# A bigger ring of exp buffers and a moved fold chunk in a kernel of attention and a spectral filter

## The chip, the cores and the metric

One core of a Trainium2 chip runs the whole program. The metric is the device time of one execution in microseconds (us). The time before is the median of three runs, 407.62 us (407.6 to 410.17). The five engines (TensorE or PE, VectorE or DVE, ScalarE or ACT, GpSimd or POOL, SyncE or SP) run side by side, each in its own order of instructions; the order is written out when the program is built, and semaphores keep the engines in step.

## The reference

Two independent halves, written side by side into one output of 2048 x 896:

```python
# A: x [1, 2048, 448], 16 heads of 28
qkv = (x @ wqkv) split into q, k, v and heads
p = softmax(q @ k^T * 28 ** -0.5)          # 16 heads x 2048 x 2048
a = (p @ v, heads side by side) @ wo
# B: x [1, 2048, 448], w_r and w_i [2048, 225]
X = rfft2(x in float32) * (w_r + 1j * w_i)
b = irfft2(X, s=(2048, 448)) as bfloat16
out = concatenate([a, b], axis=-1)
```

## The kernel before, in words

**Attention.** The 16 heads stand in four groups g of four, the 2048 queries in four chunks n of 512. A *block* is a group with a query chunk (16 blocks); a block has 16 key chunks of 128, and a key chunk four heads. A *unit* is one head's 128 keys x 512 queries of scores: 1024 units. One unit is one matmul of `fill` (L1101) into one of the eight PSUM banks. Most units are exponentiated on ScalarE (`fill_act`, L1135), one, two or three adjacent banks by one instruction, into `ET`, a ring of `ESL` = 16 buffers; `e_alloc` (L987) gives out adjacent buffers, and four matmuls (`emit_pv`, L1237) that add one key chunk of all four heads to the block's accumulator free them. For some key chunks (`KDS`) VectorE may do the exp instead: it turns scores into an integer that, read as bfloat16, is nearly the exp (L1145, tile `T`), and makes three shifted copies of four such units at once (L1158, tile `TC`); TensorE then runs four PV passes for them in place of one. Such a set of four units is called a quad here. A job that runs on TensorE in several steps is finished before a PV step may follow.

**Ahead of it**, x is transposed on TensorE against an identity table (`cid`) into `xAT`, and q, k and V of each group are projected (`proj_qk`, `proj_v`); VectorE empties them into `qT`, `kT` and `Vaug`. The start (`head`, L1371 on) does that for the first 512 rows after a few warm-up matmuls (`warm`, L1368). The denominators travel through DRAM on SP's queue (`spread`, L1270): out, back transposed, reciprocal on VectorE, out, broadcast into `rzb` by four DMAs; GpSimd then multiplies (L1286) into `onrm`.

**The spectral half** folds x by its symmetries on GpSimd (`fold_chunk`, four chunks, `fold_edge`; all by the helper `tt`, L607), multiplies by tables `FR` along the rows (`s_job`) and `T1` along the columns (`x_job`), multiplies by the weights on GpSimd (`zmul_`), goes back along the rows (`i_job`, `combine`) and by table `T2` along the columns (`y_job`). The 16 output tiles of this half (`y_job`) and the 16 of attention (`o_job`, with `Wo`) are emptied by `store` (L1341) and sent out by SP or ACT.

**The order** is made by a planner at build time, which keeps a clock for each engine and costs for each operation. ScalarE's next fill goes first, then PV steps, then jobs by due time; `FILLER` and `FORCE` put idle matmuls (L969) where TensorE would rest. Work for VectorE and GpSimd is deferred with a due time (`defer`, `flush`). `rules` (L913) draws some limits (how far VectorE may be behind, `dve`; how far ahead of ScalarE to fill, `lead`) by the seeds in `PLAN`, one for each 32 units. `HPACE` paces the loads of B's x by units done. GpSimd's operations and VectorE's `TC` copies pass one token (`port=True`): each waits by a semaphore for the last of the other engine's.

Of the kernel before, what the change touches and what calls it, by code (L numbers as in the profile page):

```python
# [23 lines left out]
class Prog:  # L24

    def __init__(self, nc, sems):
# [97 lines left out]
    def dma(self, eng, fn, sem, reads=(), writes=(), kb=128, issue=0.6, past=()):  # L124
# [193 lines left out]
def build_kernel(nc, A_x, A_wqkv, A_wo, B_x, B_w_r, B_w_i, out):  # L318
    WARM = 9
# [22 lines left out]
    with ctx:  # L342
        sem_names = ["pe", "act", "dve", "pool"]
        sem_names += ["d_x%d" % i for i in range(4)] + ["d_w", "d_wq", "d_w2", "d_wv", "d_wo", "d_c", "d_t", "d_xe"]
        sem_names += ["d_n%d" % i for i in range(7)] + ["d_i"] + ["d_xr%d" % i for i in range(4)] + ["d_wr%d" % i for i in range(2)]
# [1369 lines left out]
```

## Time and profile before

| | |
|---|---|
| median of three runs | 407.62 us |
| the profiled execution | 408.68 us, of which 406.9 us span from first to last instruction |
| PE busy | 392.0 us (96%) |
| DVE busy | 323.0 us (79%) |
| ACT busy | 385.8 us (95%), of it 379.7 us exp |
| POOL busy | 168.0 us (41%) |
| granted TensorE clock | 0.999 of full speed |
| DMA | 18.09 MB, mean 44 GB/s |

Busy is the time in which an engine has an instruction running; an instruction that overlaps the next is longer than the distance between their starts. PE's time holds the idle matmuls of L969. ACT starts its exp at 9.36 us and the rest of its time, up to 395.5 us, is nearly all exp; behind it comes the end of the last block and the last output tiles.

### The profile page before, as it was taken

Reading aid. Unit: us, or ns where it says so; the run is one execution under the profiler, and the core shown is the slowest. Engines: PE = TensorE matmul, PEld = TensorE weight load, DVE = VectorE, ACT = ScalarE, POOL = GpSimd, SP = SyncE. Lnnn points to the kernel's source line nnn. Section 1 sums busy time; section 2 is a strip of 40 time slices with the busy share of each in tenths; the row PEclk is TensorE's granted clock in tenths of the full one; section 3 lists DMA queues with packets and bytes.
Section 4 is the critical chain, followed back from the end, with each engine's and each line's share of the span. In section 5 each row is a group of like instructions: output and inputs, shape, how many; then the busy total and the mean of one; then the engine's idle time right before and its main releaser. Section 6 shows DMA issues by size and latency. Waiting matters only on the chain.

```text
span 406.9 us, 15403 instructions
## 1 busy us (share of the span) xinstructions
PE 392.0 (96%) x6693; PEld 141.4 (35%) x6693; DVE 323.0 (79%) x593; ACT 385.8 (95%) x374; POOL 168.0 (41%) x154
## 2 busy tenths in 40 slices
PE   8899999989999999999999999999999999999997
PEld 4434333333322333342424433433222224323333
DVE  2477878776899889887886788788998888979744
ACT  3899999999999999999999999999999997999992
POOL 5266674756501012465557455745225350410010
PEclk9999999999999999999999999999999999999999
DMA  8613410010000004100001400000000010021033
GB/s 243 193 55 119 143 57 6 21 37 3 17 4 15 2 15 108 48 2 4 16 3 39 130 15 3 4 17 2 15 2 16 2 17 3 27 71 47 25 104 129
DMA packets 20813, 18.09 MB, mean 44 GB/s; under 512 B 9419, under 2 KB 19593, under 8 KB 20361
## 3 DMA queue, kind: packets, MB, share of 16 engines
q1 hardware_dynamic: 18104, 13.91, 11.7%
q0 software_dynamic: 320, 1.84, 1.5%
q10 hardware_dynamic: 2320, 1.35, 1.1%
q8 instruction: 53, 0.87, 0.9%
q14 instruction: 16, 0.12, 0.1%
HBM read 13.30 MB, written 3.79 MB: 42 GB/s over the span
## 4 chain that ended last, share of the span: by engine, by line
PE 48%; ACT 42%; issue 5%; DMA 2%; DVE 2%; POOL 0%; SPq 0%; ACTq 0%; DVEq 0%; POOLq 0%
ACT ET L1135 42%; PE PS L1101 14%; PE PS L458 13%; PE PS L1237 12%; PE PS L498 5%; PE PS L969 2%; DMA R1b<-in_B_w_i_dram 1%; DMA cid<-cst_id 1%; PE PS L476 1%; PE PS L1394 0%; POOL ptmp L607 0%; PE PS L1379 0%; DVE qT L509 0%; DVE wst L1349 0%; DVE TC L1158 0%
## 5 line engine op out<-in xcount | busy, mean ns | idle before, releaser
L1135 ACT ACTIVATE ET<-PS 128x1024 bf16<-128x1024 f32 (+2 forms) x364 | 379.7, 1220 | 7.1 <-PE PS L1101 5.2
L1145 DVE TENSOR_SCALAR T<-PS 128x512 int16<-128x512 f32 x196 | 132.5, 686 | 29.3 <-PE PS L1101 27.9
L1101 PE MATMUL PS<-qT,kT 28*128 28x512 bf16 x1024 | 141.1, 384 | 5.8 <-ACT ET L1135 2.5
L1158 DVE TENSOR_SCALAR TC<-T 128x2048 int16<-128x2048 int16 x147 | 94.0, 686 | 8.7 <-POOL ptmp L607 3.6
L1101 PEld LDWEIGHTS PS<-qT,kT 28*128 28x128 bf16 x1024 | 35.2, 90 | 127.8 <-ACT ET L1135 93.3
L1237 PE MATMUL PS<-ET,Vaug 128*32 128x512 bf16 x828 | 77.0, 384 | 1.6 <-ACT ET L1135 0.8
L1286 POOL TENSOR_TENSOR onrm<-oaug,rzb 128x512 bf16<-128x512 bf16 x15 | 17.4, 1157 | 86.6 <-DVE TC L1158 39.0
L1237 PE MATMUL PS<-TC,Vs 128*32 128x512 bf16 x588 | 51.5, 384 | 0.3 <-DVE TC L1158 0.2
L458 PE MATMUL PS<-T,R 112*32 112x225 bf16 (+5 forms) x776 | 38.8, 294 | 0.6 <-DVE qT L509 0.5
L498 PE MATMUL PS<-xAT,wst 112*28 112x512 bf16 x480 | 36.9, 382 | 0.4 <-ACT ET L1135 0.4
L607 POOL TENSOR_TENSOR R<-R1b 113x512 bf16<-113x512 f32 (+1 forms) x16 | 19.9, 1280 | 32.1 <-DVE R1b L775 32.1
L607 POOL TENSOR_TENSOR ptmp<-R1a,R1b 128x450 f32<-128x450 bf16 x24 | 23.0, 972 | 23.2 <-DVE TC L1158 13.9
L1237 PEld LDWEIGHTS PS<-ET,Vaug 128*32 128x32 bf16 x828 | 20.1, 94 | 31.5 <-issue 17.2
L1349 DVE CAST wst<-PS 128x448 bf16<-128x448 f32 x26 | 16.0, 620 | 11.8 <-PE PS L458 11.2
L458 PEld LDWEIGHTS PS<-T,R 112*32 112x32 bf16 (+3 forms) x776 | 17.2, 96 | 15.8 <-issue 9.7
L607 POOL TENSOR_TENSOR ptmp<-ptmp 128x450 f32<-128x450 f32 x16 | 18.1, 1144 | 9.7 <-DVE Vs L529 4.9
L607 POOL TENSOR_TENSOR R1a<-ptmp 128x450 bf16<-128x450 f32 x16 | 15.6, 980 | 14.8 <-DVE TC L1158 8.9
L458 PE MATMUL PS<-FR,R1b 128*32 128x512 bf16 (+3 forms) x256 | 21.3, 384 | 0.2 <-issue 0.2
L969 PE MATMUL PS<-cid 128*32 128x256 bf16 x436 | 20.9, 274 | 0.6 <-ACT ET L1135 0.2
L607 POOL TENSOR_TENSOR R1b<-onrm 128x896 bf16<-128x896 f32 x8 | 16.7, 2097 | 10.5 <-DVE TC L1158 6.7
L607 POOL TENSOR_TENSOR ptmp<-R1a 128x448 f32<-128x448 bf16 (+1 forms) x16 | 16.1, 1030 | 11.1 <-DVE Vs L529 5.8
L607 POOL TENSOR_TENSOR onrm<-ptmp 128x896 f32<-128x896 f32 x8 | 17.1, 2148 | 8.3 <-DVE TC L1158 4.6
(81 smaller groups left out, 321.2 us busy)
## 6 DMA issues: line engine op xcount, KB each, us to landing
FR<-cst_tab SPq DMA_DIRECT2D x3, 1024.0 KB, 4.9
out_dram<-wst SPq DMA_DIRECT2D x26, 112.0 KB, 1.7
rzb<-scr SPq DMA_DIRECT2D x60, 32.0 KB, 1.8
R<-in_A_x_dram SPq DMA_DIRECT2D x3, 448.0 KB, 4.5
R1a<-in_B_x_dram SPq DMA_DIRECT2D x2, 448.0 KB, 3.6
out_dram<-wst ACTq DMA_DIRECT2D x6, 112.0 KB, 2.1
wst<-in_A_wqkv_dram SPq DMA_DIRECT2D x2, 294.0 KB
R<-in_A_x_dram ACTq DMA_DIRECT2D x1, 448.0 KB, 5.1
```

What stands on the lines that cost most here:

```text
L458: ins = e.matmul(out[c:c1], lhsT[:, c:c1], rhs, start=start, stop=stop, tile_position=(0, c))
L476: f = lambda e, cc=cc, i=i, dlo=dlo: e.transpose(M.bitcast(BF16)[0:112, 512 * cc + 128 * i:512 * cc + 128 * i + 128], xa[:, n, i, dlo:dlo ...
L498: ins = e.matmul(M[32 * j:32 * j + DH], wst[0:112, c, off + DH * j:off + DH * j + DH], xAT[0:112, c, 512 * n:512 * (n + 1)], start=c == 0, ...
L607: P.defer(eng, lambda e: e.tensor_tensor(out, a, b, op), reads=reads, writes=writes, busy=c, allow=allow, port=True, after=after)
L969: ins = e.matmul(PS[32 * c:32 * c + 32, 512 * b + h:512 * b + h + 256], cid[:, 32 * c:32 * c + 32] if bks else zt[:, :], cid[:, 0:256], st ...
L1101: ins = e.matmul(bank(bk), kT[32 * j:32 * j + DH, g % 2, 128 * kc:128 * (kc + 1)], qT[32 * j:32 * j + DH, b % QSL, :], start=True, stop=Tr ...
L1135: P.op("act", lambda e: e.activation(dst, src, ACT.Exp, scale=ESC), reads=[("B", i) for i in o], writes=[("E", p + k) for k in range(n)], ...
L1145: P.defer("dve", lambda e, bk=bk, slot=slot: e.tensor_scalar(T0[:, slot, :], bank(bk), BIAS, 0.0, ALU.add, ALU.max), reads=[("B", bk)], wr ...
L1158: P.defer("dve", lambda e, c=c, m=m, s0=s0: e.tensor_scalar(TC[:, c - 1, 4 * m:4 * m + 4, :], T0[:, s0:s0 + 4, :], SHF * c, None, ALU.add) ...
L1237: ins = e.matmul(bank(bk)[32 * j:32 * j + 32, :], lh, rhs, start=first, stop=last, tile_position=(0, 32 * j))
L1286: P.defer("pool", lambda e: e.tensor_tensor(onrm[:, g, cs], oaug[:, i, :], rzb[:, :], ALU.mult), reads=[ko] + [("rzb", j) for j in range(4 ...
L1349: evac(lambda e: e.tensor_copy(astg[:, slot, :], M[:, 0:448]), mk, w, 448, 1.5, after=lambda: out_dma(row, slot))
```

## The change

1. The ring `ESL` has 24 buffers in place of 16.
2. The tables `T2` and `Wo` no longer have tiles of their own: they lie in `xAT`, and are loaded by `last_loads` when the last projection has been emptied. `rzb` is gone: the reciprocals are broadcast into `onrm`, where GpSimd multiplies them in place.
3. Of the four fold chunks one (`FOLDV`) is done by VectorE, in scratch tiles that lie in `FR`; the tables for `FR` are loaded when that chunk is done. VectorE's fold operations don't pass the token.
4. A's x is loaded with four consecutive rows in a partition (3584 B in a run) in place of one (896 B); output rows follow that order. The identity table is loaded first on ACT's queue in place of second on SP's. Warm-up: 8 matmuls in place of 9, on a broadcast column of `zt`.
5. A q or k tile that is among the next that the exp needs (`wanted`) is due for emptying at once (-3.0 in place of 1.0).
6. The planner: landing times are kept by semaphore; `dve` may be drawn from 1.0 to 4.0 in place of 2.0 to 3.0; up to two VectorE units in a fill (`ndf`) in place of one (`NDF`); new seeds; B's x is asked for at units 2 and 5 in place of 3 and 13.

```diff
-ESL = 16
+ESL = 24
...
+FOLDV = (3,)
+FALLOW = {"dve": 12.0, "pool": 12.0}
...
-HPACE = ((3, "x", 0), (5, "w", 1), (5, "x", 1), (5, "w", 0))
+HPACE = ((2, "x", 0), (3, "x", 1), (5, "w", 1), (5, "w", 0))
...
-    WARM = 9
+    WARM = 8
...
-        wo = sb("wo", [128, NG, 448])
...
-        T2 = sb("T2", [128, 2, 2, D])
...
-        rzb = sb("rzb", [128, 512])
...
+        T2 = xflat[:, 0:1792].rearrange("p (v b k) -> p v b k", v=2, b=2)
+        wo = xflat[:, 1792:3584].rearrange("p (g k) -> p g k", g=NG)
...
-            P.dma(q, lambda e, n=n: e.dma_start(xa[:, n], A_x[0][512 * n:512 * n + 512, :].rearrange("(c p) d -> p c d", p=128)),
+            P.dma(q, lambda e, n=n: e.dma_start(xa[:, n], A_x[0][512 * n:512 * n + 512, :].rearrange("(p c) d -> p c d", p=128)),
                   "d_x%d" % n, writes=[("xa", n)], kb=448)
         load_x(0)
-        P.dma("sp", lambda e: e.dma_start(cid[:, :], cst_h.ap()[:, :]), "d_c", writes=["cid"], kb=32)
+        P.dma("act", lambda e: e.dma_start(cid[:, :], cst_h.ap()[:, :]), "d_c", writes=["cid"], kb=32)
...
-                evac(fn, mk, [key] + ([("k", 0, "h")] if key == ("k", 0, 0) and g else []), 512, 1.0, after=lambda: done.add(nmk))
+                def after():
+                    done.add(nmk)
+                    last_loads()
+                evac(fn, mk, [key] + ([("k", 0, "h")] if key == ("k", 0, 0) and g else []), 512, -3.0 if nmk in wanted() else 1.0, after=after)
...
+        def last_loads():
+
+            if st.get("last") or any((k, NG - 1, n) not in done for k in "qkV" for n in range(4)):
+                return
+            st["last"] = True
+            xk = [k for n in range(4) for k in xkeys(n)]
+
+            def load_o():
                 for j in range(4):
                     P.dma("sp", lambda e, j=j: e.dma_start(wo[32 * j:32 * j + DH, :, :], A_wo.rearrange("(g j d) n -> j d g n", g=NG, j=4)[j]),
-                          "d_wo", reads=["wo"], past=rd, writes=[("wo", j)], kb=98)
+                          "d_wo%d" % j, reads=["wo"], writes=[("wo", j)], kb=98)
+            P.dma("sp", lambda e: e.dma_start(T2, t2_h.ap()[:, :].rearrange("p (v b k) -> p v b k", v=2, b=2)), "d_t", writes=["T2"] + xk, kb=448)
+            P.defer("pool", lambda e: e.memset(wo, 0.0), writes=["wo"] + xk, busy=1.6, allow=6.0, port=True, after=load_o)
...
-            P.defer(eng, lambda e: e.tensor_tensor(out, a, b, op), reads=reads, writes=writes, busy=c, allow=allow, port=True, after=after)
+            P.defer(eng, lambda e: e.tensor_tensor(out, a, b, op), reads=reads, writes=writes, busy=c, allow=allow, port=eng == "pool", after=after)
...
+        def folded():
+
+            st["folded"] = st.get("folded", 0) + 1
+            if st["folded"] == 2 * len(FOLDV):
+                own = [("L0", "dve", h, x) for h in range(2) for x in "abc"] + [("L1", "dve"), ("L1", "dve", 1)]
+                load_f(0, 0, (), own)
+                load_f(1, 1, (), own)
...
-                    "dve": r.choice((2.0, 2.5, 3.0)) if p else 2.5,
+                    "dve": r.choice((1.0, 2.0, 2.5, 3.0, 4.0)) if p else 2.5,
+                    "ndf": r.choice((1, 1, 2)) if p else 1,
...
+        def wanted():
+
+            r = set()
+            for k in (0,) + QKL:
+                if k < a_left():
+                    r.update(want_qk(*au(st["ai"] + k)[:2]))
+            return r
...
-                    P.dma("sp", lambda e, j=j: e.dma_start(rzb[32 * j:32 * j + 32, :], scr[1, i, 512 * j:512 * j + 512].unsqueeze(0).to_broadcast([32, 512])),
-                          "d_n%d" % (3 + j), reads=[("scr", 1, i)], writes=[("rzb", j)], kb=32, issue=0.1)
-                P.defer("pool", lambda e: e.tensor_tensor(onrm[:, g, cs], oaug[:, i, :], rzb[:, :], ALU.mult), reads=[ko] + [("rzb", j) for j in range(4)],
...
+                    P.dma("sp", lambda e, j=j: e.dma_start(onrm[32 * j:32 * j + 32, g, cs], scr[1, i, 512 * j:512 * j + 512].unsqueeze(0).to_broadcast([32, 512])),
+                          "d_n%d" % (3 + j), reads=[("scr", 1, i)], writes=[("rzb", g, qc, j)] + (old if j == 0 else []), kb=32, issue=0.1)
+                P.defer("pool", lambda e: e.tensor_tensor(onrm[:, g, cs], oaug[:, i, :], onrm[:, g, cs], ALU.mult), reads=[ko] + [("rzb", g, qc, j) for j in range(4)],
...
-            pe_op("full", lambda e: e.matmul(bank(b), onrm[:, 3, 1536:1664], onrm[:, 3, 1536:2048], start=True, stop=True), ["zero"], [("B", b)], dur)
+            pe_op("full", lambda e: e.matmul(bank(b), zt[:, 0:1].to_broadcast([128, 128]), zt[:, 0:1].to_broadcast([128, 512]), start=True, stop=True), ["zt"], [("B", b)], dur)
...
-                    fold_chunk("pool", c, 12.0)
+                    fold_chunk("dve" if c in FOLDV else "pool", c, FALLOW["dve" if c in FOLDV else "pool"])
...
-                        while rest and len(used) < 4 and len(sel) < NDF and P.backlog("dve") + 0.9 * len(sel) < rules()["dve"]:
+                        while rest and len(used) < 4 and len(sel) < rules()["ndf"] and P.backlog("dve") + 0.9 * len(sel) < rules()["dve"]:
```

## Rows read from the trace of the kernel before

**Rows 1.** Groups by shape, ScalarE's exp: count | busy us, mean ns of one.
```profile
L1135 ACT ACTIVATE ET<-PS 128x1024 bf16<-128x1024 f32 x242 | 237.1, 1108 | 2.5 <-PE PS L1101 1.5 <-ACT ET L1135 0.6
L1135 ACT ACTIVATE ET<-PS 128x1536 bf16<-128x1536 f32 x111 | 164.7, 1525 | 4.4 <-PE PS L1101 3.5 <-PE PS L476 0.5
...
L1135 ACT ACTIVATE ET<-PS 128x512 bf16<-128x512 f32 x11 | 6.7, 610 | 0.3 <-PE PS L1101 0.2
```

**Rows 2.** Chain of waits, 165 to 168 us: start us, length us, what.
```profile
165.42 0.71 ACT ET L1135
...
166.32 1.11 ACT ET L1135
...
167.65 0.88 ACT ET L1135
```

**Rows 3.** Timeline of the head: start us, us, instruction, [idle before, what ended it].
```profile
1.19 4.02 PE L1369 MATMUL PS<-onrm 128*128 128x512 bf16 x9 [1.19 <-DVE zt L433]
4.74 0.34 SPq L427 DMA_DIRECT2D wv<-in_A_wqkv_dram  x1
5.32 1.57 PEld L1379 LDWEIGHTS PS<-cid,R 128*112 128x112 bf16 x16 [1.02 <-DMA cid<-cst_id]
...
9.36 4.21 ACT L1135 ACTIVATE ET<-PS 128x1536 bf16<-128x1536 f32 x3 [0.58 <-PE PS L1101]
```

**Rows 4.** ScalarE's timeline from 336 us on, behind the longest gap.
```profile
342.05 53.46 ACT L1135 ACTIVATE ET<-PS 128x1536 bf16<-128x1536 f32 x51 [2.08 <-PE PS L1101]
```

**Rows 5.** Groups by shape up to 340.9 us: exp on ScalarE, PV matmuls that read ET.
```profile
L1135 ACT ACTIVATE ET<-PS 128x1024 bf16<-128x1024 f32 x208 | 204.8, 1113 | 2.4 <-PE PS L1101 1.5 <-ACT ET L1135 0.6
L1135 ACT ACTIVATE ET<-PS 128x1536 bf16<-128x1536 f32 x95 | 142.0, 1529 | 2.3 <-PE PS L1101 1.4 <-PE PS L476 0.5
L1135 ACT ACTIVATE ET<-PS 128x512 bf16<-128x512 f32 x10 | 6.1, 609 | 0.3 <-PE PS L1101 0.2
...
L1237 PE MATMUL PS<-ET,Vaug 128*32 128x512 bf16 x696 | 64.4, 384 | 1.6 <-ACT ET L1135 0.8
```

**Rows 6.** Timeline near 232 us: TensorE behind a q tile's emptying.
```profile
232.08 0.97 PE L458 MATMUL PS<-T,R 113*32 113x225 bf16 x32 [0.53 <-DVE qT L509]
```

**Rows 7.** Timelines: GpSimd's first and last fold, first spectral matmul; GpSimd's L607, 20 to 112 us.
```profile
23.29 3.98 POOL L607 TENSOR_TENSOR ptmp<-R1a 128x448 f32<-128x448 bf16 x4 [5.24 <-DVE R1a L1420]
27.61 2.14 POOL L607 TENSOR_TENSOR onrm<-ptmp 128x896 f32<-128x896 f32 x1
...
108.62 1.13 POOL L607 TENSOR_TENSOR R1b<-ptmp 1x448 bf16<-1x448 f32 x1 [0.88 <-DVE TC L1158]
...
112.09 0.61 PE L458 MATMUL PS<-FR,R1b 128*32 128x512 bf16 x8 [0.17 <-issue]
...
20.00:112.00 92.00, 54.09 (x36) 1.00 0.17 52
```

**Rows 8.** Filler matmuls of L969 by window: stretch, us, PE busy, PEld busy, clock, DMA.
```profile
80.00:120.00 40.00, 11.19 (x232) 4.69 (x232) 1.00 0.06 16
```

**Rows 9.** PE, PEld, DVE, ACT, POOL in one window; TensorE's output tiles after 396 us.
```profile
352.00:396.00 44.00, 43.87 (x625) 13.71 (x625) 32.48 (x55) 43.80 (x43) 2.31 (x2) 1.00 0.18 56
...
L458 PE MATMUL PS<-wo,onrm 128*32 128x448 bf16 x128 | 6.4, 353 | 0.0
L458 PE MATMUL PS<-T,R 113*32 113x448 bf16 (+1 forms) x32 | 1.8, 353 | 0.0
```

**Rows 10.** DMA issues: count, KB each, median us from issue to landing.
```profile
R1a<-in_B_x_dram SPq DMA_DIRECT2D x2, 448.0 KB, 3.6
...
R<-in_A_x_dram SPq DMA_DIRECT2D x3, 448.0 KB, 4.5
```

**Rows 11.** Groups by shape, VectorE: exp, shifted copies, tensor_tensor with a PSUM operand.
```profile
L1145 DVE TENSOR_SCALAR T<-PS 128x512 int16<-128x512 f32 x196 | 132.5, 686 | 29.3 <-PE PS L1101 27.9
L1158 DVE TENSOR_SCALAR TC<-T 128x2048 int16<-128x2048 int16 x147 | 94.0, 686 | 8.7 <-POOL ptmp L607 3.6 <-POOL R L607 2.6 <-POOL R1b L607 1.5
...
L775 DVE TENSOR_TENSOR R1b<-R1b,PS 113x512 f32<-113x512 f32 x4 | 2.7, 684 | 1.2 <-DVE rz L1296 0.7 <-PE PS L458 0.6
```

More of the change, by code (lines that the diff above doesn't have):

```diff
@@ L41, in __init__ @@
         self.port = (None, None, 0.0)
+        self.land = {}
         self.hist = {e: {} for e in ENG}
@@ L98, in ready @@
             if w is not None and not (eng == "pe" and w[0] == "pe"):
-                t = max(t, w[1])
+                t = max(t, self.land.get(w[0], w[1]))
         for k in writes:
@@ L102, in ready @@
                 if r != eng:
-                    t = max(t, e)
+                    t = max(t, self.land.get(r, e))
         return t
@@ L134, in dma @@
         self.dma_free = max(self.dma_free, start + issue) + kb / 220.0
-        self._mark("dma", ev, reads, writes, self.dma_free + 2.0)
+        self.land[sem] = self.dma_free + 2.0
+        self._mark(sem, ev, reads, writes, self.land[sem])
     def blocked(self, reads, writes):
@@ L343, in build_kernel @@
         sem_names = ["pe", "act", "dve", "pool"]
-        sem_names += ["d_x%d" % i for i in range(4)] + ["d_w", "d_wq", "d_w2", "d_wv", "d_wo", "d_c", "d_t", "d_xe"]
-        sem_names += ["d_n%d" % i for i in range(7)] + ["d_i"] + ["d_xr%d" % i for i in range(4)] + ["d_wr%d" % i for i in range(2)]
+        sem_names += ["d_x%d" % i for i in range(4)] + ["d_w", "d_wq", "d_w2", "d_wv", "d_c", "d_t", "d_xe"]
+        sem_names += ["d_n%d" % i for i in range(7)] + ["d_wo%d" % i for i in range(4)] + ["d_i"] + ["d_xr%d" % i for i in range(4)] + ["d_wr%d" % i for i in range(2)]
         sem_names += ["d_xb%d" % i for i in range(4)] + ["d_f%d" % i for i in range(2)] + ["d_wb%d" % i for i in range(4)] + ["d_o%d" % i for i in range(NST)]
@@ L525, in scaled @@
                 late_loads(g, n)
+                last_loads()
                 for ki, kc in enumerate(KDS):
@@ L578, in mirrored @@
                 src = (B_w_r, B_w_i)[r]
-                old = ["zero", ("L1", "pool"), ("L1", "pool", 1)] if h == 0 else []
+                old = [("L1", "pool"), ("L1", "pool", 1)] if h == 0 else []
                 P.dma("sp", lambda e: e.dma_start(Wmir[h][:, r], src[1024:2048, :].rearrange("(p m q) k -> p m q k", m=4, q=2)[:, :, h, :]), "d_wb%d" % (2 * h + r),
@@ L618, in fold_chunk @@
                 tt(eng, l[:, :, 225:448], x[:, :, 1:224], x[:, :, 447:224:-1], B, xk, [k0 + (h, "b")], 446, allow)
-                P.defer(eng, lambda e, l=l, x=x: e.tensor_copy(l[:, :, 0:1], x[:, :, 0:1]), reads=xk, writes=[k0 + (h, "c")], busy=0.2, allow=allow, port=True)
+                P.defer(eng, lambda e, l=l, x=x: e.tensor_copy(l[:, :, 0:1], x[:, :, 0:1]), reads=xk, writes=[k0 + (h, "c")], busy=0.2, allow=allow, port=eng == "pool")
             k0 = [k0 + (h, x) for h in range(2) for x in "abc"]
@@ L622, in fold_chunk @@
             tt(eng, l1[:, 1::2, :], l0[:, 0::2, :], l0[:, 1::2, :], B, k0, [k1 + (1,)], 896, allow)
-            tt(eng, fh[:, :, 448 * c:448 * c + 448], l1[:, 0:2, :], l1[:, 2:4, :], A, [k1, k1 + (1,)], [("f", 0, c)], 896, allow)
-            tt(eng, fh[:, :, 1792 + 448 * c:1792 + 448 * c + 448], l1[:, 0:2, :], l1[:, 2:4, :], B, [k1, k1 + (1,)], [("f", 1, c)], 896, allow)
+            for k, op in ((0, A), (1, B)):
+                tt(eng, fh[:, :, 1792 * k + 448 * c:1792 * k + 448 * c + 448], l1[:, 0:2, :], l1[:, 2:4, :], op, [k1, k1 + (1,)], [("f", k, c)], 896, allow, after=folded if eng == "dve" else None)
+        def folded():
[4 more added lines that the diff above has]
+                load_f(1, 1, (), own)
         def fold_edge(allow):
@@ L1353, in part @@
                 return [mm(M[:, 0:448], onrm[:, g, 512 * qc + 128 * tl:512 * qc + 128 * tl + 128], wo[:, g, :], g == 0, g == NG - 1) for g in gs]
-            r0 = 512 * qc + 128 * tl
-            end = lambda M, mk: store(out[0, r0:r0 + 128, 0:448], M, mk)
+            r0 = 512 * qc + tl
+            end = lambda M, mk: store(out[0, r0:r0 + 509:4, 0:448], M, mk)
             wk = [("wo", j) for j in range(4)]
@@ L1534, in build_kernel @@
                 pl = plan_fill(now)
-                for k in (0,) + QKL:
-                    if k < a_left():
-                        urgent.update(want_qk(*au(st["ai"] + k)[:2]))
+                urgent.update(wanted())
                 if pl is None:
```

22 lines of the change are left out of this document (8 added, 14 removed).

## The prediction

> **What bounds the kernel now.** I began with the first part of the page. ScalarE and TensorE are both busy nearly throughout, so I asked which of them sets the pace. The groups of ScalarE by shape show that it does the exp in 242 pairs, 111 triples and 11 single score tiles, 828 of the 1024 units [rows 1]; VectorE does the other 196, that is 49 sets of four ("quads"). In a stretch without waits the chain of waits runs along ScalarE alone: a pair starts 0.90 us before the next instruction, a triple 1.33 us [rows 2]. At that pace the work is 242 x 0.90 + 111 x 1.33 + 11 x 0.61 = 372.1 us. It starts at 9.36 us [rows 3] and ends at 342.05 + 53.46 = 395.5 [rows 4], so 386.1 us pass and some 14 us are lost. The whole is then a head of 9.4 us, 372 us of exp, 14 us of stalls and a tail of 11.4 us to 406.9. TensorE's busy time holds filler matmuls on purpose, so its share proves nothing by itself; where it is truly full is the end, 43.87 of 44 us from 352 to 396 [rows 9].
>
> **The profiled execution** took 408.68 us, 1.06 us above the median 407.62 of the runs. I add changes to its rows and subtract the same sum from the median.
>
> **Head: -0.7 us.** The transposes start at 5.32 us, after 1.02 us of waiting for the identity table, which was issued behind the first quarter of x on SP [rows 3]. That quarter had landed by 4.74, since SP's next load waits for it [rows 3]. With the table first on ACT's queue it is no longer last. The warm-up ended at 1.19 + 4.02 = 5.21; one matmul fewer (0.45 us) and no 0.3 us fill of its operand put its end at 4.5. So 0.6 us (x as before) to 0.8 us (TensorE's own warm-up). Two weight loads and one x load move behind the table's issue on ACT's queue, about 0.5 us each; no wait for them shows now, so I give them nothing, and 0.5 us if they are late next. Four-row runs: A's x takes 4.5 us to land in one-row runs, B's x of the same size 3.6 us in four-row runs [rows 10], so up to 0.9 us, most of it hidden by the warm-up. The Trainium skill, DMA: Bandwidth & Descriptors, Specifications, asks for at least 512 B for line rate, which 896 B rows already have; by that the runs are worth nothing and this term is 0.6.
>
> **Ring of exp buffers: -3.5 us.** Before the longest stall, up to 340.9 us, ScalarE had done 208 x 2 + 95 x 3 + 10 = 711 units and TensorE had consumed 696 matmuls / 4 heads = 174 sets = 696 units [rows 5]: 15 of 16 buffers held, while a long side job kept the PV matmuls back. ScalarE then waited for scores, 2.1 us [rows 4]; over the run it waits 1.5 + 3.5 + 0.2 = 5.2 us for them [rows 1]. Eight more buffers are 3.6 us of exp, enough to cover that one whole. Lower end -2.1 (this gap alone), upper -5.2 (all). I take the middle; what could be late next is the PV work pushed back, at a time at which TensorE is running filler.
>
> **Urgent keys: -0.5 us.** Near 232 us TensorE stands 0.53 us for a q tile to be emptied [rows 6]. Ends 0 and the rest of the small losses, 2 us.
>
> **Fold: earlier spectral work, tail -2.5 us.** GpSimd folds from 23.29 to 109.75 us, and the first spectral matmul follows at 112.09; its operations are 54.09 us busy in that stretch [rows 7]. Less the edge (about 4 us), a chunk is 12.5 us of work, and at that duty (54.1 of 86.5 us) 20 us of time. Three chunks, and x fetched 8 units earlier (8 x 0.45 = 3.6 us), bring the first spectral matmul to about 88 us. From 80 to 120 us TensorE runs 11.2 us of filler for want of work [rows 8]; that is where the spectral matmuls go. What this frees lies at the end: after 396 us TensorE still has 6.4 us for eight output tiles of the attention half and 1.8 us for two of the spectral half [rows 9], and only the last four attention tiles need the last exp. So 6.4 / 2 + 1.8 = 5.0 us at most, 0 at least, half as forecast. The tables F now load after VectorE's chunk; nobody needs them before the fold ends. T2 and Wo wait for the last projections, which every output tile already waits for; their loads take a few us where DMA is nearly idle: nothing, or 3 us if an output tile is due at once. The in-place broadcast takes the same four DMAs on SP as before; for the last head group SP also waits for the old W tiles, long read by then: nothing, or one output DMA's delay.
>
> **Price of the fold on VectorE: +1.0 us.** Eight tensor_tensors of 448 or 896 columns at 684 ns per 512 [rows 11] are 4 x 0.60 + 4 x 1.20 = 7.2 us, with two copies 7.6. Behind each in VectorE's order wait score evacuations, then TensorE's banks, then ScalarE. The port that GpSimd and VectorE share was reserved by semaphores; VectorE waits for it now in front of its copies [rows 11]. The new fold takes it without asking. No row shows a collision: from below nothing (neither is slowed, so no gain either), from above eight times the longest GpSimd operation, 2.14 us [rows 7], 17 us. I take 59% (54.09 of 92 us busy) x 8 x 0.65 = 3 us of waiting, a third of it reaching ScalarE, since the window has idle time on VectorE. The Trainium skill, SBUF — State Buffer, Who interferes with whom, says that a VectorE instruction with two SBUF inputs and a GpSimd one that reads SBUF exclude each other for the whole instruction; that speaks against this part, and at its worst gives the third rival below.
>
> **Share of VectorE: -1.8 us.** A quad costs VectorE 4 x 0.686 + 3 x 0.686 = 4.8 us [rows 11] and saves ScalarE 4 x 0.45 = 1.8. If the fold displaces its own time, 1.6 quads go back: +2.9 us. If the looser limits (up to two units a fill, backlog up to 4.0) fill what VectorE idles ahead of scores, 27.9 us less 7.6 [rows 11], 4.2 quads come over: -7.6 us. I take one quad more, nearer the first, since the seeds are new choices and not a rule to fill. The landing times by semaphore change only the planner's picture: nothing by themselves.
>
> **Sum**: -0.7 - 3.5 - 0.5 - 2.5 + 1.0 - 1.8 = -8.0 us. The profiled execution would take 400.7, the median **399.6 us**. A measurement tells about 1% from no change: faster is below 403.5, slower above 411.7.
>
> **Rivals.** *More goes to VectorE* (chance 0.12): half of the 27.9 us filled, 14 / 4.8 = 2.9 quads instead of one, 3.4 us more: 396.2, down to 393 with all 4.2. For it: VectorE idles there because TensorE offers no score tile, which two a fill would change. Against: each quad costs TensorE three more PV passes.
>
> *The gain comes back at the end* (0.20): the deeper ring only delays PV matmuls, which TensorE does later, and the last stretch is full [rows 9]. Ring and tail then give nothing, nor does the quad: 407.62 - 0.7 - 0.5 + 1.0 = 407.4, with parts of either 403.5 to 409. It is also the case in which the ring, though larger, was not what held ScalarE. Against it stands the count of 15 held buffers.
>
> *The port* (0.09): each of the eight operations stands for a GpSimd operation of 2.1 us, and all but the 0.65 us by which the planner fills ahead reaches ScalarE: 8 x 1.45 = 11.6 us in place of 1.0, 410.2; at the full 17 us 415.6. It ends slower than before from 9.0 us on, slower by 1% from 13.1 on. For it: GpSimd is busy more than half of that stretch. Against: only one chunk in four moves, and VectorE has idle time there.
>
> **Chances.** My forecast, within 394 to 403.4, has 0.59. Faster by over 1%: 0.59 + 0.12 = 0.71; the same 0.21, most of the second rival and half of the port; slower 0.08. The range takes in the first rival and most of the second: 393 to 407.
>
> **What the next profile should show.** Head: the first exp at 8.7 instead of 9.36. Ring: no gap of 2 us in ScalarE's waits for scores, and more than 16 units held now and then. Fold: the first spectral matmul near 88 us, little filler from 80 to 120 us, GpSimd's fold operations in three quarters of their number. Tail: four attention tiles, and no spectral ones, after the last exp. Quads: 48 to 53 sets of T and TC. Port: the tensor_tensors of the fold on VectorE, or GpSimd's beside them, longer than 0.6 and 1.2 us. I am wrong if the ScalarE stretch from first to last exp stays at 386 us, or if the tail keeps its 11 us though spectral work begins 20 us earlier.

## The result, and the profile after

| | before | after |
|---|---|---|
| median | 407.61 us (407.56 to 410.17) | 413.86 us (413.44 to 415.39) |
| ratio | | 1.0145, interval 1.0098 to 1.0192 |
| profiled execution, its span | 408.68 us, 406.9 us | 413.75 us, 411.9 us |
| first exp to last (start to end) | 9.36 to 395.5: 386.1 us | 8.92 to 403.9: 395.0 us |
| behind the last exp | 11.4 us | 8.0 us |

The change makes the kernel 1.45% slower (by the ratio); 399.6 us was forecast. One of the ten executions of experiment 1 below (412.11 us) ran in the chip's slower state: its median of 407.31 us counts it, its ratio does not, and without it the median is 406.89 us. Head and tail improved by 0.4 and 3.4 us, and the stretch of ScalarE's exp grew by 8.9 us. That growth isn't spread out: from 20 to 60 us ScalarE is busy 30.65 of 40 us, where the kernel before has this row (the same view: stretch; busy us and instructions of PE, PEld, DVE, ACT, POOL; clock, DMA share, GB/s):

```profile
20.00:60.00 40.00, 38.73 (x758) 15.15 (x758) 30.63 (x64) 40.00 (x39) 26.02 (x22) 1.00 0.28 89
```

The windows of the changed kernel, with the stretch of [rows 9] at the end:

```profile
20.00:60.00 40.00, 35.04 (x637) 12.68 (x636) 33.78 (x57) 30.65 (x29) 21.05 (x17) 0.83 0.22 71
...
32.00:36.00 4.00, 2.08 (x56) 0.82 (x48) 3.96 (x2) 2.80 (x3) 3.92 (x3) 1.00 0.06 18
36.00:40.00 4.00, 2.91 (x45) 1.17 (x49) 3.97 (x4) 1.48 (x2) 4.00 (x2) 0.64 0.00 0
40.00:44.00 4.00, 3.16 (x27) 0.51 (x19) 4.00 (x4) 2.45 (x2) 1.17 (x1) 0.50 0.00 0
44.00:48.00 4.00, 4.00 (x37) 0.90 (x33) 1.87 (x10) 2.41 (x2) 0.88 (x1) 0.50 0.63 225
48.00:52.00 4.00, 4.00 (x86) 1.62 (x82) 2.34 (x4) 2.80 (x4) 3.37 (x6) 0.66 0.60 180
...
352.00:396.00 44.00, 43.84 (x639) 14.04 (x628) 36.16 (x62) 43.73 (x41) 1.38 (x2) 1.00 0.20 61
```

Two things are to be seen: from 32 to 44 us VectorE is full with very few instructions (ten in 12 us), and from 36 to 52 us the granted clock is 0.5 to 0.66, TensorE's lower level of 1.2 GHz for most of it, also while TensorE is busy all the time. The timeline of the changed kernel says which instructions these are; the head stands ahead of them ([rows 3]), the first spectral matmul and the end behind ([rows 7, 4]):

```profile
4.75 1.84 PE L1408 MATMUL PS<-cid,R 128*112 128x128 bf16 x16 [0.22 <-DMA R<-in_A_x_dram]
...
8.92 1.45 ACT L1163 ACTIVATE ET<-PS 128x1536 bf16<-128x1536 f32 x1 [0.58 <-PE PS L1129]
...
24.97 9.83 ACT L1163 ACTIVATE ET<-PS 128x1024 bf16<-128x1024 f32 x9 [0.94 <-PE PS L1129]
...
31.15 4.25 POOL L618 TENSOR_TENSOR onrm<-ptmp 128x896 f32<-128x896 f32 x2
31.54 1.79 DVE L630 CAST FR<-R1a 128x2 f32<-128x2 bf16 x1
...
33.36 2.98 DVE L618 TENSOR_TENSOR FR<-FR 128x896 f32<-128x896 f32 x1
...
35.47 5.70 POOL L618 TENSOR_TENSOR R1b<-onrm 128x896 bf16<-128x896 f32 x2
36.27 0.68 DVE L511 TENSOR_SCALAR kT<-PS 128x512 bf16<-128x512 f32 x1
36.87 2.36 DVE L618 TENSOR_TENSOR FR<-FR 128x896 f32<-128x896 f32 x1
...
37.09 0.61 PE L1129 MATMUL PS<-qT,kT 28*128 28x512 bf16 x3 [3.01 <-DVE kT L511]
...
37.81 1.45 ACT L1163 ACTIVATE ET<-PS 128x1536 bf16<-128x1536 f32 x1 [3.01 <-PE PS L1129]
...
39.26 2.86 DVE L618 TENSOR_TENSOR R1b<-FR 128x896 bf16<-128x896 f32 x1
...
42.05 0.68 DVE L511 CAST qT<-PS 128x512 bf16<-128x512 f32 x1
...
42.78 1.47 PE L500 MATMUL PS<-xAT,wst 112*28 112x512 bf16 x12 [0.84 <-DVE qT L511]
43.18 1.07 DVE L618 TENSOR_TENSOR R1b<-FR 128x896 bf16<-128x896 f32 x1
...
44.90 1.45 ACT L1163 ACTIVATE ET<-PS 128x1536 bf16<-128x1536 f32 x1 [1.95 <-PE PS L1129]
...
62.52 2.08 POOL L618 TENSOR_TENSOR R1b<-onrm 128x896 bf16<-128x896 f32 x1
...
100.10 0.39 PE L460 MATMUL PS<-FR,R1b 128*32 128x512 bf16 x4
...
399.72 4.20 ACT L1163 ACTIVATE ET<-PS 128x1536 bf16<-128x1536 f32 x4
```

Read it from 31 us on. GpSimd folds its first chunk (two operations of 2.1 us, then two of 2.85) while VectorE folds chunk 3. VectorE's operations of 896 columns take 2.98, 2.36 and 2.86 us as long as GpSimd's run beside them, and 1.07 us at 43.18, when GpSimd is done; GpSimd's last two take 2.85 us on average beside them, and 2.08 us alone (62.52). In VectorE's order the emptying of a `kT` tile stands behind the first of them and that of a `qT` tile behind the third. TensorE waits 3.01 us for `kT`, ScalarE the same 3.01 us for its scores.

The groups of the changed kernel: exp on ScalarE and quads on VectorE over the whole run ([rows 1, 11]), VectorE's fold from 20 to 60 us, filler from 80 to 120 us ([rows 8]; the row's last columns are clock and DMA), and the output tiles after 404 us ([rows 9]; all 84 matmuls are of attention):

```profile
L1163 ACT ACTIVATE ET<-PS 128x1024 bf16<-128x1024 f32 x255 | 247.0, 1123 | 4.1 <-PE PS L1129 3.2 <-PE PS L1265 0.8
L1163 ACT ACTIVATE ET<-PS 128x1536 bf16<-128x1536 f32 x101 | 149.7, 1517 | 8.1 <-PE PS L1129 7.5 <-PE PS L1265 0.3
...
L1173 DVE TENSOR_SCALAR T<-PS 128x512 int16<-128x512 f32 x196 | 131.8, 685 | 31.9 <-PE PS L1129 30.3 <-issue 0.4
...
L618 DVE TENSOR_TENSOR FR<-FR 128x896 f32<-128x896 f32 x2 | 5.3, 2672 | 0.0
...
80.00:120.00 40.00, 4.73 (x88) 1.87 (x88) 1.00 0.04 9
...
L460 PE MATMUL PS<-xAT,onrm 128*32 128x448 bf16 x84 | 4.9, 353 | 0.1
```

There are 49 quads as before (196 units), so VectorE's share didn't move. ScalarE waits 11.5 us for scores in place of 5.2.

### The profile page after: what moved, and what is told of

Same layout as the page of the kernel before. It is cut to its first block, busy times and chain, and to the rows that moved or that the text cites. A ratio compares the mean times of both kernels' runs of the same rounds, so it can differ in the third digit from the quotient of the medians.

```text
span 411.9 us, 15025 instructions
## 1 busy us (share of the span) xinstructions
PE 395.0 (96%) x6500; PEld 136.4 (33%) x6500; DVE 336.0 (82%) x605; ACT 386.9 (94%) x378; POOL 156.9 (38%) x144
## 3 DMA queue, kind: packets, MB, share of 16 engines
q1 hardware_dynamic: 17240, 14.19, 11.7%
q10 hardware_dynamic: 1648, 1.07, 0.9%
## 4 chain that ended last, share of the span: by engine, by line
ACT 44%; PE 40%; DVE 7%; issue 5%; DMA 2%; POOL 1%; SPq 0%; ACTq 0%; POOLq 0%; DVEq 0%
ACT ET L1163 44%; PE PS L1129 12%; PE PS L460 11%; PE PS L1265 10%; PE PS L500 4%; DVE FR L618 2%; PE PS L989 1%; DMA R<-in_A_x_dram 1%; DMA scr<-rz 1%; DVE TC L1186 1%; DVE T L1173 1%; DVE R1b L618 1%; DVE FR L630 1%; PE PS L478 1%; DVE kT L511 0%
## 5 line engine op out<-in xcount | busy, mean ns | idle before, releaser
L1163 ACT ACTIVATE ET<-PS 128x1024 bf16<-128x1024 f32 (+2 forms) x371 | 382.4, 1209 | 13.1 <-PE PS L1129 11.5
L1129 PE MATMUL PS<-qT,kT 28*128 28x512 bf16 x1024 | 145.0, 389 | 7.4 <-DVE kT L511 3.2
L1315 POOL TENSOR_TENSOR onrm<-oaug,onrm 128x512 bf16<-128x512 bf16 x15 | 17.3, 1155 | 119.4 <-DVE TC L1186 58.4
L500 PE MATMUL PS<-xAT,wst 112*28 112x512 bf16 x480 | 40.6, 403 | 2.1 <-DVE qT L511 0.8
L460 PE MATMUL PS<-T,R 112*32 112x225 bf16 (+2 forms) x520 | 21.4, 263 | 0.0
L460 PE MATMUL PS<-wv,xAT 112*32 112x112 bf16 x1024 | 21.1, 216 | 0.3 <-DVE xAT L486 0.3
L618 POOL TENSOR_TENSOR ptmp<-R1a 128x448 f32<-128x448 bf16 (+1 forms) x12 | 12.5, 1050 | 20.8 <-DVE Vs L535 16.2
L460 PE MATMUL PS<-FR,R1a 128*32 128x512 bf16 (+2 forms) x256 | 20.2, 383 | 0.0
L1265 PE MATMUL PS<-T,Vaug 128*32 128x512 bf16 x196 | 19.2, 383 | 0.0
L460 PEld LDWEIGHTS PS<-wv,xAT 112*32 112x32 bf16 x1024 | 15.0, 97 | 10.0 <-issue 6.9
```

The source lines that it names most:

```text
L460: ins = e.matmul(out[c:c1], lhsT[:, c:c1], rhs, start=start, stop=stop, tile_position=(0, c))
L500: ins = e.matmul(M[32 * j:32 * j + DH], wst[0:112, c, off + DH * j:off + DH * j + DH], xAT[0:112, c, 512 * n:512 * (n + 1)], start=c == 0, ...
L618: P.defer(eng, lambda e: e.tensor_tensor(out, a, b, op), reads=reads, writes=writes, busy=c, allow=allow, port=eng == "pool", after=after)
L1129: ins = e.matmul(bank(bk), kT[32 * j:32 * j + DH, g % 2, 128 * kc:128 * (kc + 1)], qT[32 * j:32 * j + DH, b % QSL, :], start=True, stop=Tr ...
L1163: P.op("act", lambda e: e.activation(dst, src, ACT.Exp, scale=ESC), reads=[("B", i) for i in o], writes=[("E", p + k) for k in range(n)], ...
L1265: ins = e.matmul(bank(bk)[32 * j:32 * j + 32, :], lh, rhs, start=first, stop=last, tile_position=(0, 32 * j))
```

## The experiments

Each was timed against the kernel before on the same chip; medians of before lay between 407.18 and 407.62 us, so a difference of two medians below can be off by some tenths; where it matters the difference of the ratios is given too. The collision of the fold is the theory; the rivals were that the redrawn order, the ring or the later spectral tables cost the time.

**1. The token back.** VectorE's fold operations wait for GpSimd's by the semaphore of the shared port, and the planner plans with it.

```diff
-            P.defer(eng, lambda e: e.tensor_tensor(...), ..., port=eng == "pool", after=after)
+            P.defer(eng, lambda e: e.tensor_tensor(...), ..., port=True, after=after)
```

> The changed kernel, but VectorE's fold operations pass the token too, so that no fold operation of one engine runs beside one of the other. The planner lays the order out anew. Port theory (VectorE's fold operations stand for GpSimd's on the shared port, keys come late, TensorE rests, its clock falls): the 896-column operations take about 1.1 us instead of 2 to 3, ScalarE is busy at least 37 of the 40 us from 20 to 60 (30.65 in the changed kernel), granted clock 1.0 there, median 403 to 407 us. Work theory (7 us of fold are too much for VectorE at that time, with or without the port): ScalarE still loses 6 us or more there, median 410 us or more. Plan theory (the new order is bad elsewhere): no change in 60 to 400 us and a median that stays above 409.

Measured: 407.31 us, ratio 0.9999 (0.9962 to 1.0036). The fold's 896-column operations on VectorE take 1.08 us again; in the window of this kernel the clock is 1.00 and ScalarE is busy 39.14 us of 40:

```profile
20.00:60.00 40.00, 38.77 (x811) 14.66 (x796) 32.43 (x69) 39.14 (x39) 21.27 (x19) 1.00 0.09 24
```

The loss is gone, but so is the gain.

**2. The same order, GpSimd quiet.** GpSimd's first chunk (c = 0), the one beside VectorE's, only fills its targets with zeros, so the spectral half isn't computed from it; every wait and the order stay.

```diff
-            P.defer(eng, lambda e: e.tensor_tensor(out, a, b, op), ...)
+            P.defer(eng, (lambda e: e.memset(out, 0.0)) if quiet else lambda e: e.tensor_tensor(out, a, b, op), ...)
+            quiet = eng == "pool" and c == 0
```

> The changed kernel in the same order of instructions, but GpSimd's first fold chunk only fills its outputs with zeros (it reads nothing; the spectral half is then not the reference's). VectorE's fold work stays as it is. Port theory: VectorE's tensor_tensors take 0.6 and 1.1 us, its two small copies under 0.2 us, no 3 us gap of TensorE near 34 us, clock 1.0 throughout, ScalarE busy 38 us or more in 20 to 60, median 403 to 406 us. Work theory: the operations may be shorter, but ScalarE still loses 5 us or more in 20 to 60, median 410 to 414.

Measured: 402.29 us, ratio 0.9885 (0.9863 to 0.9906), a little faster than either expectation. The window, the groups and, from ScalarE's timeline, the same exp that starts at 24.97 us in the changed kernel:

```profile
20.00:60.00 40.00, 39.05 (x821) 14.69 (x809) 34.98 (x72) 39.45 (x37) 19.57 (x22) 1.00 0.23 77
...
L618 DVE TENSOR_TENSOR FR<-FR 128x896 f32<-128x896 f32 x2 | 2.2, 1086 | 0.0
L618 POOL MEMSET onrm<- 128x896 f32 x2 | 1.6, 846 | 0.1
...
22.99 47.76 ACT L1164 ACTIVATE ET<-PS 128x1024 bf16<-128x1024 f32 x45 [0.39 <-PE PS L1130]
```

With nothing changed but what GpSimd does beside it, VectorE's operation takes 1086 ns in place of 2672, the clock stays at 1.00, and the whole is 413.86 - 402.29 = 11.6 us faster (10.6 by the ratios). The collision is shown, and everything else in the change is worth -1.15% in this order. Two reservations: GpSimd's first chunk is also shorter here (fills of 0.85 us for operations of 2.1), which puts the first spectral matmul at 89.1 in place of 100.1 us. And not all of the difference is the collision: of the 11.0 us between the two spans (411.9 and 400.9), 2.0 lie ahead of VectorE's first fold operation (25.21 us), since the exp that starts at 24.97 us in one starts at 22.99 in the other; in the first kernel of experiment 5, whose order is the same up to there, it starts at 23.31.

**3. The price by itself.** A kernel with nothing but VectorE and GpSimd: eight VectorE operations of each kind, alone, beside GpSimd's tensor_tensors, beside its fills.

```diff
+        read(10)   # GpSimd: tensor_tensor 128x896 f32, both inputs in SBUF
+        for i in range(N): V(lambda e, i=i: e.tensor_tensor(vo[:, i, :], va[:, :], vb[:, :], ALU.add))
+        fill(14)   # GpSimd: memset 128x896 f32
+        for i in range(N): V(...)   # and so on for the other kinds
```

> Not the kernel: the disputed collision by itself (the output is zeros). On VectorE eight each of: tensor_tensor of two SBUF tiles 128x896 float32, copies of 128x2 bfloat16 to float32, emptying copies of a 128x512 PSUM tile, int16 tensor_scalars 128x2048 in SBUF; each alone, beside GpSimd tensor_tensors 128x896 that read SBUF, and beside GpSimd fills that only write. Port theory: tensor_tensor about 1.0 to 1.1 us alone and beside fills, 2 to 3 us beside GpSimd's reads; the emptying copies from PSUM 0.68 us in all three. Work theory: the tensor_tensors take about the same in all three.

Measured once. Groups of this kernel; L61, L72, L83 and L94 run alone, L65, L76, L87 and L98 beside GpSimd's tensor_tensors, L69, L80, L91 and L102 beside its fills:

```profile
L65 DVE TENSOR_TENSOR vo<-va,vb 128x896 f32<-128x896 f32 x8 | 21.2, 2720 | 0.0
L98 DVE TENSOR_SCALAR to<-ta 128x2048 int16<-128x2048 int16 x8 | 18.0, 2322 | 0.0
L102 DVE TENSOR_SCALAR to<-ta 128x2048 int16<-128x2048 int16 x8 | 10.7, 1406 | 6.1 <-POOL po L54 6.1
L61 DVE TENSOR_TENSOR vo<-va,vb 128x896 f32<-128x896 f32 x8 | 8.1, 1086 | 9.0 <-POOL z L50 9.0
...
L69 DVE TENSOR_TENSOR vo<-va,vb 128x896 f32<-128x896 f32 x8 | 8.1, 1085 | 6.1 <-POOL po L54 6.1
...
L94 DVE TENSOR_SCALAR to<-ta 128x2048 int16<-128x2048 int16 x8 | 4.9, 687 | 1.9 <-POOL po L58 1.9
L87 DVE CAST eo<-ps 128x512 bf16<-128x512 f32 x8 | 4.9, 682 | 0.0
...
L76 DVE CAST vd<-vc 128x1 f32<-128x1 bf16 x8 | 0.6, 145 | 0.0
```

The copies ran as 128x1, not 128x2 as expected above. The fold's operation costs 1.09 us alone and 2.72 beside GpSimd's reads: 1.63 us more. Beside fills it costs nothing more. The Trainium skill, SBUF — State Buffer, Who interferes with whom, says that a VectorE operation with two SBUF inputs contends with a GpSimd one that reads SBUF and not with one that only writes it: 2720 against 1085 ns bears that out. PSUM emptying (682 ns) isn't touched, so it can't be the collision itself that delays `kT`: it is its place behind a fold operation.

**4. Explicit waits, same order.** Like 1, but the planner doesn't know of the waits, so the order stays.

```diff
-        self._emit_waits(eng, reads, writes, self.port[1] if port and ...)
+        self._emit_waits(eng, reads, writes, self.tok[1] if (port or soft) and ...)
```

> The changed kernel in the same order of instructions, but VectorE's fold operations and GpSimd's wait for each other by semaphores; the planner still takes them to run side by side. Port theory: a wait in front of the operation is as long as the wait inside it, so ScalarE still loses 8 us or more in 20 to 60 and the median is 411 to 417 us; what helped the kernel with the token was the planner's knowledge. If the collision itself costs more than the exclusion (both slowed while they overlap): 403 to 409 us.

Measured: 411.97 us, ratio 1.0107 (1.0056 to 1.0159); the interval overlaps that of the change. VectorE's operations take 1.09 us each, and the time has become waits; ScalarE loses 6.1 us from 20 to 60 in this execution, not 8. VectorE's waits of this kernel from 20 to 60 us (who <- for whom: us, times, longest), and its window:

```profile
DVE FR L634 <- POOL onrm L622: 1.9, 1, 1.9
DVE FR L622 <- POOL onrm L622: 1.6, 1, 1.6
DVE FR L634 <- POOL ptmp L622: 1.2, 1, 1.2
DVE R1b L622 <- POOL R1b L622: 1.1, 1, 1.1
...
20.00:60.00 40.00, 38.00 (x681) 13.83 (x679) 29.17 (x60) 33.94 (x32) 21.93 (x19) 0.83 0.20 70
```

1.9 + 1.6 + 1.2 + 1.1 = 5.8 us of waits stand where the long operations stood, the clock falls to the same 0.83 in this execution, and most of the loss remains: 9.7 of 11.6 us by the medians. So a longer operation and a wait in front of it come out about alike, as long as VectorE works through GpSimd's chunk in this order. How the loss reaches ScalarE is less clear here: TensorE shows no wait of 3 us but two shorter ones (1.1 and 0.7 us), after which its clock is 0.50 from 32 to 44 us; the three executions without a profile kept a mean clock of 0.991 to 0.996 and took 411.4 to 413.2 us all the same.

**5. The clock.** Idle matmuls where TensorE waits, in the order of the change: 104 (26 times four) ahead of the score matmul that waits for `kT`; then a second kernel with 104 more ahead of the projection that waits for `qT`.

```diff
+            def idle(e):
+                for i in range(26):
+                    for c in range(4):
+                        ins = e.matmul(PS[32 * c:32 * c + 32, ...], zt[:, :], cid[:, 0:256], start=False, stop=False, tile_position=(0, 32 * c))
+            P.streams["pe"].append(idle)
```

> The changed kernel in the same order, with 104 idle matmuls (about 2.8 us at full clock) put ahead of the score matmul that waits 3 us for a key tile, so that TensorE does not rest there. Nothing else changes; the lock on the port stays. If the fallen clock is a large share of the loss: the clock stays at 1.0 to 40 us at least and ScalarE loses 4 to 7 us in 20 to 60 in place of 10, median 408 to 411 us. If the clock is a side effect: ScalarE loses 9 us or more there, median 413 to 415.

Measured: 411.4 us, ratio 1.0096 (1.0067 to 1.0126), overlapping the change and between the two expectations. The first wait no longer lowers the clock, the next one does. Windows and timeline of this kernel:

```profile
36.00:40.00 4.00, 2.21 (x48) 0.60 (x33) 3.97 (x2) 3.61 (x3) 3.49 (x2) 1.00 0.01 4
40.00:44.00 4.00, 2.90 (x27) 0.85 (x31) 2.87 (x5) 0.79 (x1) 0.00 (x0) 0.55 0.14 16
```

```profile
41.09 1.47 PE L501 MATMUL PS<-xAT,wst 112*28 112x512 bf16 x12 [2.89 <-DVE qT L512]
```

> The changed kernel in the same order, with 104 idle matmuls (four at a time, some 5 us of TensorE) ahead of the score matmul that waits for kT at 34 us and 104 more ahead of the projection that waits for qT at 38 to 41 us. The granted clock should stay at 1.00 from 20 to 60 us. The waits for VectorE stay as they are. If the half clock carries 4 to 5 us of the 11.6 that the collision costs, the time is 408 to 410; if the waits alone do, and the slow matmuls lay beside them, 411 to 413.9, with ScalarE still near 31 us busy from 20 to 60. If the idle matmuls delay what stands behind them, over 414.

Measured: 410.13 us, ratio 1.0063 (1.0045 to 1.0080), below the interval of the change and just over the first expectation. Window of this kernel:

```profile
20.00:60.00 40.00, 38.89 (x898) 18.38 (x897) 36.62 (x61) 34.02 (x33) 25.10 (x19) 1.00 0.21 69
```

ScalarE's waits for scores from 20 to 60 us, in the changed kernel, in this one and in the quiet one of 2 (us, times, longest):

```profile
ACT ET L1163 <- PE PS L1129: 9.3, 10, 3.0
ACT ET L1178 <- PE PS L1143: 5.9, 4, 2.8
ACT ET L1164 <- PE PS L1130: 0.6, 2, 0.4
```

The clock's share is 413.86 - 410.13 = 3.7 us (3.3 by the ratios), in ScalarE's busy time 34.02 - 30.65 = 3.4, in its waits 9.3 - 5.9 = 3.4. The waits for VectorE with the clock held up are 5.9 - 0.6 = 5.3 us of ScalarE's time. By the medians 410.13 - 402.29 = 7.8 us are left (7.3 by the ratios); the 2 us and more beyond 5.3 lie outside the collision, in part ahead of it (experiment 2), and aren't explained further.

**6. The ring.** The quiet kernel of 2 with 16 buffers, the planner's order following from the same seeds.

```diff
-ESL = 24
+ESL = 16
```

> The changed kernel with GpSimd's first chunk only filling zeros (402.29 us with 24 buffers) and 16 exp buffers; the order is planned anew, with seeds drawn for the other order. Ring theory of the prediction: 3.5 us slower (404.4 to 407.5), with gaps of ScalarE of 0.5 us and more at 14 or 15 held buffers. If the ring hardly mattered: 401 to 403.5, and no such gaps.

Measured: 410.04 us, ratio 1.0064 (1.0041 to 1.0087), 7.75 us slower than with 24, the intervals apart, and outside both expectations. ScalarE's waits for scores rise from 2.9 to 9.5 us. This kernel's row of waits:

```profile
ACT ET L1164 <- PE PS L1130: 9.5, 14, 1.6
```

**7. The urgent keys.** The quiet kernel with the old due time.

```diff
-                evac(..., 512, -3.0 if nmk in wanted() else 1.0, after=after)
+                evac(..., 512, 1.0, after=after)
```

> The changed kernel with GpSimd's first chunk only filling zeros (402.29 us), and the old due time for all q and k tiles; the order is planned anew. Prediction: 0.5 us slower, up to 2 us. If the new order alone moves it by more than 2 us either way, seeds weigh more than this part.

Measured: 404.12 us, ratio 0.9903 (0.9870 to 0.9937). 1.8 us slower by the medians; the intervals overlap, and the order is another too, so this part can't be told from nothing.

**8. All four chunks on GpSimd**, the rest of the change kept.

```diff
-FOLDV = (3,)
+FOLDV = ()
...
+                load_f(0, 0, rd)
...
+                load_f(1, 1, rd)
```

> The changed kernel with all four fold chunks on GpSimd and the F tables loaded where the kernel before loads them; all other parts of the change stay. Port theory: ScalarE is busy 38 us or more in 20 to 60, the first spectral matmul comes near 110 us, median 402 to 406 us. If another part of the change (ring, late tables, x in runs, key order, seeds) makes it slower: 410 us or more.

Measured: 408.61 us, ratio 1.0044 (1.0027 to 1.0061), between the two expectations. ScalarE is busy 39.73 of 40 us from 20 to 60; 14.0 us pass behind the last exp. With nothing moved to VectorE there is no collision and no half clock from 20 to 60 us; the time is lost at the end. That this is so because the first spectral matmul comes at 111.1 us in an order made for an earlier one is a guess that experiment 9 fits (8.3 us behind the last exp with new seeds).

**9. Seeds of their own.** Runs 1, 6 and 8 had to use seeds of `PLAN` that had been found for the change. Here the seeds are searched for each kernel by itself: the token (as 1), all on GpSimd (as 8), and the token with 16 buffers.

```diff
-PLAN = [99474, 1186, 90693, 47638, 0, 35866, 75804, 3167, ...]
+PLAN = [99474, 0, 90693, 47638, 0, 32126, 61399, 3167, ...]   # token; others for the other two
```

> The change with the token given back to VectorE's fold operations (as in the run with the token, which took 407.31 us and was as fast as before), and with the order drawn anew from other seeds of PLAN. If the collision at the port is all that the change does wrong, and the token's 407.31 was an unlucky order drawn for other costs, it comes near the quiet kernel's 402.3: 398 to 403 us. If the token itself costs VectorE's fold the 5 us that lie between 402.3 and 407.3 (operations that wait for GpSimd one after the other), no seed helps and it stays at 405 to 409. Either way the fold's 896-column operations are at 1.1 us, ScalarE is busy 39 of 40 us from 20 to 60 us and the clock is 1.00 there.

> All four fold chunks on GpSimd as before the change, the rest of the change kept, and the order drawn anew (with the changed kernel's seeds it took 408.6). If moving a chunk to VectorE brings nothing by itself, this is as fast as the token with new seeds, within 1.5 us. If the chunk on VectorE is worth the earlier spectral work (tail -2.5 us in the prediction), it is 2 to 5 us slower than that, 401 to 406, with the first spectral matmul near 110 us in place of 90 to 100 and a tail over 9 us.

> The token with a ring of 16 exp buffers again, the order drawn anew for it. With the deeper ring worth what the prediction gave it (3.5 us) it is 3 to 4 us slower than the token with 24 buffers and new seeds; with the 7.75 us that the quiet kernel lost by 16 buffers and seeds drawn for 24, 7 to 8 slower; if that loss was the seeds' and not the ring's, within 1.5 us of it.

| | median | ratio, interval | first spectral matmul | behind the last exp |
|---|---|---|---|---|
| token, 24 buffers | 402.95 us | 0.9884 (0.9855 to 0.9914) | 99.3 us | 9.8 us |
| all on GpSimd, 24 buffers | 403.63 us | 0.9906 (0.9881 to 0.9931) | 113.9 us | 8.3 us |
| token, 16 buffers | 403.79 us | 0.9917 (0.9899 to 0.9936) | 94.3 us | 8.3 us |

All three beat the kernel before by 0.8 to 1.2%, and the change by more, and their intervals overlap each other. With an order made for it, the ring of 16 costs 0.8 us by the medians and not 7.75, and the chunk on VectorE brings 0.7; neither can be told from nothing. Of the kernels that compute everything, the first, the token with its own seeds, has the lowest median.

**10. The kernel before with new seeds only.**

```diff
-PLAN = [0, 46211, 67299, 93510, 67638, 0, 0, 0, 3501, ...]
+PLAN = [0, 46211, 67299, 0, 67638, 0, 32329, 21197, 3501, ...]
```

> The kernel before, with nothing changed but the seeds of PLAN, drawn anew in the same way as for the three kernels with their own seeds (402.95, 403.63 and 403.79 us). If those three are faster than before because of what they keep of the change (head, urgent keys, limits, tables loaded late), this stays at 406.5 to 408.5. If drawing the order anew is what brings their 1%, and the parts of the change bring nothing beyond it, it comes to 402.5 to 404.5. Between the two, 404.5 to 406.5, both have a share.

Measured: 406.14 us, ratio 0.9970 (0.9945 to 0.9994). New seeds alone bring 0.3%. The three of 9 are 2.4 to 3.2 us faster than this; so much is left for what they share with the change: head, urgent keys, tables loaded late, looser limits, x of B asked for earlier. Which of these has how much isn't shown, nor how far another search for seeds would land from this one.

## Why the prediction was wrong, point by point

**Price of the fold on VectorE: +1.0 us** is the step that failed. It took 3 us of waiting at the port, "a third of it reaching ScalarE, since the window has idle time on VectorE". Both factors were wrong, and a term was missing.

- *The waiting.* VectorE's eight tensor_tensors take 11.7 us and its copies 2.8, 14.5 in all where 7.6 was forecast: 6.9 us of waiting, inside the bounds (0 to 17), over twice the value taken. The 59% by which the bound was scaled down assumed that the two engines meet by chance. They don't: both wait for x of B and then start 1.7 us apart (23.47 and 25.21 us), so VectorE's chunk falls on GpSimd's first.
- *What reaches ScalarE.* 5.3 us of the 6.9 with the clock held up, three quarters and not a third. VectorE's idle time lies elsewhere in the window; between 31.5 and 42 us its order is fold operation, `kT`, fold, fold, `qT`, and TensorE waits for both tiles. The prediction had named those queued behind (score evacuations) and then let an average over the window hide them.
- *The clock.* The prediction had no term for it. While TensorE rests for these tiles the granted clock falls to 0.5, and that costs another 3.4 us of ScalarE's time (3.7 by the medians).

Together 5.3 + 3.4 = 8.7 us in ScalarE's waits, and up to 11.6 by the medians, in place of 1.0. The third rival, *the port*, had the mechanism and by its own working 8 x 1.45 = 11.6 us; that this equals the difference of the medians is luck, since it held no clock and gave all eight operations the same wait, where the four of 448 and 446 columns took 0.61 us and waited for nothing. Its "against" was the mistake: one chunk in four is moved, but it is the one that meets the other. A chance of 0.09 for it was too low. The rule of the Trainium skill (SBUF — State Buffer, Who interferes with whom) that was cited as speaking against this part, that such a pair of instructions excludes each other, is borne out by the 2720 against 1086 ns of experiment 3.

**The other terms** came to -9.0 us; without the collision, they are 402.29 - 407.18 = -4.9 (before on the same chip).

- *Head, -0.7:* the wait for `cid` is gone, as forecast, and the transposes start at 4.75 when x lands (before: 5.32). The first exp is at 8.92, 0.44 us earlier. In the runs with the new head it lies between 8.0 and 9.3, with the old head at 9.36 and 8.81; that spread is as large as the term.
- *Ring, -3.5:* the gap of 2 us [rows 4] is indeed gone in the quiet kernel (longest wait 0.6 us), yet counted as in [rows 5] the changed kernel never holds more than 17 of the 24 buffers. What 16 cost depends on the order: 7.75 us with seeds found for 24, 0.8 us with its own. A single gap in a trace was read as the price of the buffer; it was the price of that order.
- *Urgent keys, -0.5:* between nothing and 1.8 us; no contradiction, not more than that.
- *Tail, -2.5:* 3.4 us, and only attention tiles after the last exp, as forecast (over five in place of four). The reason given fails. GpSimd does fold less (43.4 us busy from 20 to 112, before 54.1, [rows 7]), but the first spectral matmul came at 100.1 in place of 88 us: the fold starts no earlier than before (23.47, before 23.29), though x was asked for earlier, and with GpSimd quiet the matmul comes at 89.1. And the tail doesn't follow it (8.3 us with it at 113.9, 9.8 us with it at 99.3). Filler from 80 to 120 us fell from 11.2 to 4.7 us, as expected.
- *Share of VectorE, -1.8:* nothing; 49 quads, the same.

So of *the gain comes back at the end* half held: the quad brought nothing, and the ring, in orders made for it, nothing that could be told from zero, while the tail did improve.

## What to carry to other kernels

Before moving work to an engine, look for what will run on the engine that it shares a port with at that very time, and price the meeting by what stands next in the fixed order, not by idle time averaged over a window; here the waits on the path cost about half as much again through TensorE's clock (3.7 us beside 7.8 by the medians, 3.4 beside 5.3 in ScalarE's waits). Work that may collide should lie where nothing urgent is queued behind it, and the planner should know the wait: the same token took 411.97 us in an order that didn't know of it, 407.31 in one that did, and 402.95 with seeds found for it. A part of a change can be valued only with an order made for it; with borrowed seeds the ring looked worth 7.75 us, with its own 0.8.

## What the runs showed of the hardware

- Two tensor_tensors of 128x896, VectorE's 1.09 us alone and GpSimd's 2.03 (16.26 us for eight, nearly alone: the copies beside them take 0.6 us in all), take 2.72 us as a pair when both read SBUF, a little less than one behind the other (3.12). GpSimd's is slowed too: 2.85 in place of 2.08 us in the changed kernel.
- An int16 operation of 128x2048 on VectorE with one SBUF input, like the `TC` copies, takes 687 ns alone, 2322 beside GpSimd's reads and 1406 beside its fills; so in this run fills don't slow the fold's operation, but do slow these.
- A copy of 128x1 took 145 ns alone and where GpSimd's reads ran beside it (for the last 0.4 of the 0.6 us that eight of them take), yet the fold's copies of 128x2 took 1.0 and 1.79 us in the changed kernel, 0.60 and 0.15 with GpSimd quiet, and 0.16 with the token. Copies of 128x2 weren't run by themselves.
- After TensorE had waited 3.0 us the clock fell to 0.64 and 0.50, and it stayed below 1.00 until about 51 us, with TensorE busy 2.9 to 4.0 of every 4 us meanwhile. With idle matmuls in both rests it stayed at 1.00 from 20 to 60 us.
